# Moving the first two groups' routing matmuls, the first expert's search and loads, and two units' transposes in a fused linear-attention and mixture-of-experts kernel

## The chip, the cores and the metric

The kernel runs on one core of one Trainium2 chip. The metric is the device time of one execution in microseconds (us); the time before is the median of three runs. Engines are named as the profile names them: PE is TensorE (PEld its weight loads), DVE is VectorE, ACT is ScalarE, POOL is GpSimd, and SP is SyncE, which issues most DMA transfers. TensorE runs at one of two clock levels, 2.4 or 1.2 GHz.

## The reference

Two parts follow each other. The first is a linear attention with a decaying state; its output rows are the tokens of the second, a mixture of 8 experts of which each token uses one.

```python
B, H, S, D = 4, 8, 768, 48                    # r, k, v: (B, H, S, D)
for t in range(S):
    cur = einsum('bhd,bhe->bhde', u * k_t, v_t)
    y_t = einsum('bhd,bhde->bhe', r_t, state + cur)
    state = w * state + einsum('bhd,bhe->bhde', k_t, v_t)
x = y as rows                                  # (N = 3072, DM = 384)
logits = x @ w_gate + modality_bias[modality_id]      # 8 experts, 2 modalities
e = argmax(logits); g = softmax(logits)[e]
out[n] = g * (relu(x[n] @ w1[e]) @ w2[e])      # w1: 384 x 1024, w2: 1024 x 384
```

## The kernel before

**Units and iterations.** The attention is cut into 24 units: chunk c of 128 time steps (6 of them) of batch b (4), in the order unit = 4 c + b. A hand-written loop runs over iterations i = 0 to 22, and within an iteration the code itself sets the order of every engine's queue; each engine takes its instructions strictly in that order. Iteration i works on several units at once, in this order on PE: the transposes of the finished rows of unit i - 2 (`raised`, into PSUM tile pxT, only for the units in RAISED = 6 to 11), the transposes of the keys of unit i + 2 (`keys_turned`, pkT), the scores of unit i + 1 (`scores`, psc), then the outputs of unit i (`values`: py from the state and from the masked scores at, then the new state pst, then the small matmuls of `bonus`, line 411).

**The chain of a unit's row.** In iteration i + 1 DVE adds the bonus term to py of unit i (`token`, line 509), ACT squares it and sums (line 524), DVE makes a power-of-two scale of it (ebx and sx, lines 314 and 316), ACT writes the high half of the row as fp16 (`high`, line 557), DVE the low half (`low`, line 561). DVE's queue in an iteration is: token, key scaling kc (line 402), ebx, sx, the two masked score halves at (line 456), low. Low frees one of the two py buffers. The row is then turned: for RAISED units by six PE transposes in iteration i + 2 and one ACT copy (`flipped`, line 585), for the others by a DMA transpose that SP issues at the end of iteration i + 1 (`flip`, line 577).

**Transfers.** SP issues the loads of unit i + 5's transposed inputs (ud) and of unit i + 4's keys and values (kv) in iteration i. Ahead of each stands a read of a value whose only use is the time at which it is there (`pace`): SP goes on to ud when ACT has copied d of unit i, and on to kv when DVE has written sx of unit i - 1.

**Routing.** Units form GROUPS (0 to 3, 4 to 7, 8 to 11, 12 to 15, ...). For a group that ends with unit l, PE makes its `logits` at the end of iteration l + 2 and its `count` (how many tokens go to which expert, and each token's place) at the end of iteration l + 4. DVE's parts, `choose` (pick the expert; it ends with three operations on the sum zs, lines 636 to 640) and `place`, are generators in a list `fills`: one operation of it is emitted at each call of `fill()`, between the large operations. `route(i, d, f)` calls f for the group whose last unit is i - d + 1.

**The first expert.** The biases and the token counts of the two modalities tell the order in which experts are worth loading. `setup2` and `first_order` compute it; ctl holds the result, SP reads it in iteration 6, and loads the first expert's 3 MB of weights in 12 halves (`half`, line 964), two in each of iterations 6 to 11. ACT squares and sums six pieces of them for a scale (`norm`, line 967), PE and DVE make the scale of each matrix (`scales`), and ACT and DVE split each piece into fp16 parts whi (line 998) and wlo (line 1003): piece 0 to 2 in iterations 10 to 12, pieces 3 to 5 at the end of iteration 13. The expert's matmuls are woven in from iteration 13 on (`s_up`, `s_down`), and after the attention the kernel runs expert jobs alone.

Of the kernel before, what the change touches and what calls it, by code (L numbers as in the profile page):

```python
# [9 lines left out]
F32 = mybir.dt.float32  # L10
# [5 lines left out]
ALU = mybir.AluOpType  # L16
# [30 lines left out]
TURNED = range(1, 15)  # L47
RAISED = range(6, 12)
OWNED = range(17, 24)
# [3 lines left out]
EARLY = 3  # L53
ROWS, ENDS = 5 * E, 6 * E + 4
GROUPS = ((0, 4), (4, 8), (8, 12), (12, 16), (16, 19), (19, 22), (22, 24))
MS = ('DVE', 'Activation', 'PE', 'SP', 'Pool')
# [9 lines left out]
class _Kernel:  # L66
# [134 lines left out]
    def setup2(self):  # L201
# [9 lines left out]
        yield  # L211
        pt = self.ps_r.tile([P, 512], F32, tag="r", name="pswg")
        nc.tensor.matmul(pt[:, :1], self.ones, ssq, start=True, stop=True)
# [17 lines left out]
        NTT = NT // P  # L231
        mf, mp = pt[:, 64 : 64 + NTT], c.tile([P, 1], F32, name="modp")
        self.polled = pt, mp, bias
        nc.scalar.activation(mf, mod.rearrange("p (t w) -> p t w", w=2)[:, :, 0], AF.Copy, accum_out=mp)
        yield
        mg = pt[:, 96 : 96 + NTT]
# [360 lines left out]
    def choose(self, u):  # L597
# [36 lines left out]
        yield "oh"  # L634
        zs = col(456)
        nc.vector.reduce_sum(zs, ex, axis=AX.X)
# [68 lines left out]
    def sorted(self, key, ck, n=1):  # L705
# [10 lines left out]
        return perm, rank  # L716

    def first_order(self):

        c, v = self.c, self.nc.vector  # L720
        pt, mp, bias = self.polled
        one = slice(0, 1)
        new = lambda name, shape: c.tile(shape, F32, name=name)
        b2 = bias.rearrange("p (m e) -> p m e", m=2)
        n1, rev, best1, perm = new("n1", [P, 1]), new("rev16", [P, E]), new("best1", [P, E]), new("perm0", [P, E, E])
        self.perm0 = perm
        square = lambda ap: ap.rearrange("p (a b) -> p a b", b=E)
        top, gr = pt[:, 384:386], square(pt[:, 128 : 128 + E * E])
        best0, by, rank, t = (pt[:, o : o + E] for o in range(400, 400 + 4 * E, E))
        self.nc.tensor.matmul(pt[:, 1:2], self.ones, mp, start=True, stop=True)  # L730
        v.reduce_max(top, b2, axis=AX.X)
        yield
        self.nc.scalar.activation(rev, self.rev, AF.Copy, scale=1 / 16)
        self.nc.scalar.activation(rev, self.rev, AF.Copy, scale=1 / 16)
        v.tensor_tensor(best0, b2[:, 0], top[:, :1].to_broadcast([P, E]), ALU.is_equal)
        yield
        self.nc.scalar.copy(n1, pt[:, 1:2])
        v.tensor_tensor(best1, b2[:, 1], top[:, 1:].to_broadcast([P, E]), ALU.is_equal)
        yield
        v.tensor_sub(by, best1, best0)  # L740
        yield
        v.scalar_tensor_tensor(best1, best0, float(NT), rev, ALU.mult, ALU.add)
        yield
        v.scalar_tensor_tensor(rev, by, n1, best1, ALU.mult, ALU.add)
        yield
        v.scalar_tensor_tensor(best0, by, n1, best1, ALU.mult, ALU.add)
        yield
        v.tensor_tensor(gr, rev.unsqueeze(1).to_broadcast([P, E, E]), best0.unsqueeze(2).to_broadcast([P, E, E]), ALU.is_gt)
# [12 lines left out]
        self.nc.scalar.copy(self.ctl[:, :E], eid)  # L761
# [393 lines left out]
    def run(self):  # L1155
# [26 lines left out]
        def plan(step, f):  # L1182
            at.setdefault(step, []).append(f)
# [5 lines left out]

        def half(q):  # L1190
            if q == 0:
                self.eid = nc.sync.value_load(self.ctl[:, :1], min_val=0, max_val=E - 1)
            if 0 <= q < 2 * NQ:
                self.load(self.eid, 2 * NQ, q)

# [4 lines left out]
        def chain(*gs):  # L1200
            for g in gs:
                yield from g

        routing = self.setup2()
        plan(0, lambda: next(routing))
        plan(1, lambda: next(routing))
        plan(1, lambda: fills.append(routing))
        plan(3, lambda: fill(99))
        plan(3, lambda: fills.append(self.first_order()))
        mid[5] = lambda: fill(99)  # L1210
        plan(3, lambda: nc.sync.dma_start(self.ut, self.u.to_broadcast([P, DM])))
        plan(4, lambda: nc.gpsimd.memset(self.st[0], 0.0))
# [7 lines left out]
        for q in range(NQ):  # L1220
            plan(O + 9 + q, norm(q))
        for q in range(3):
            plan(O - 1 + q, norm(q))
        begin[O + 2] = lambda: scales("w1", 0, O + 2)
        for q in range(3):
            plan(O + 2 + q, split(q))
            plan(O + 2 + q, norm(3 + q))
            plan(O + 5, split(3 + q))
        mid[O + 5] = lambda: self.values(O + 5, lambda: (scales("w2", 1, O + 6), self.undo()))
        for q in range(NQ):  # L1230
# [24 lines left out]
        for i in range(NU - 1):  # L1255
# [6 lines left out]
            if i + 1 > EARLY:  # L1262
                each(i + 1, self.own_keys)
            route(i, 3, lambda u: fills.append(self.choose(u)))
            route(i, 5, lambda u: fills.append(chain(self.place(u), self.ahead(ahead[u["lo"]], u)) if u["lo"] in ahead else self.place(u)))
# [24 lines left out]
            if 0 < i < NU - 5:  # L1290
                self.pace(self.ctx_[i]["d"])
                each(i + 5, self.turned)
            half(2 * (i - O) + 4)
            for j in range(2):
# [20 lines left out]
            if i:  # L1315
                fac = self.factor(i - 1)
                for _ in fac:
                    fill()
                if i < NU - 4:
                    self.pace(self.ctx_[i - 1]["g"]["sx"][:, self.ctx_[i - 1]["at_g"] :])  # L1320
                    each(i + 4, self.lines)
                half(2 * (i - O) + 5)
                each(i + 3, self.own_lines)
# [16 lines left out]
            fill()  # L1340
            if i != O + 5:
                self.values(i)
            if up is not None:
# [8 lines left out]
            if i != O + 4 and any(hi - 1 + d == i for lo, hi in GROUPS for d in (4, 5)):  # L1352
                fill(99)
            route(i, 2, self.logits)
            route(i, 4, self.count)
            for f in at.get(i, ()):
# [215 lines left out]
```

## Time and profile before

| | us |
|---|---|
| median of 3 runs (340.3, 342.31, 342.3) | 342.3 |
| the profiled execution, its own time | 340.73 |
| its span, first to last instruction | 338.9 |
| PE busy | 322.9 |
| DVE busy | 210.2 |
| ACT busy | 180.9 |
| POOL busy | 159.7 |

The profiled execution takes 1.8 us more than its span, and stands between the runs. All times of the profile below count from the span's start. Iteration i of the loop begins on PE with the first transposes of that iteration; iterations 1 to 4 take about 3.6 to 5 us each, iterations 5 to 12 about 5 to 8, and the attention's loop ends at about 160 us. The expert jobs fill the rest. A matmul's duration in the profile overlaps the next one's, so what PE needs for a piece of work is read from one start to the next.

### The profile page before, as it was taken

The page shows a single profiled execution, that of the slowest core. Times are in us where ns is not written, and L with a number is a line of the kernel's source. Part 1 is how long each engine was busy: PE and PEld are TensorE (multiplying, and loading weights), DVE is VectorE, ACT ScalarE, POOL GpSimd, SP SyncE. Part 2 cuts the span into 40 slices and gives each one's busy share as a digit, 9 for nine tenths or more (in the row PEclk, how much of TensorE's full clock was granted, in tenths as well). Part 3 has the DMA queues.
Part 4 walks back from the last instruction along what each step waited for, and adds up shares of the span by engine and source line. Part 5 has one row for each costly group of instructions (what it writes and reads, how often), then busy time and mean ns, then how long its engine had stood idle before and what let it go on. Part 6 is the DMA issues. An engine that isn't in the chain of part 4 may idle for free. (4 is left out here: it accounts for less than half of the span.)

```text
span 338.9 us, 15229 instructions
## 1 busy us (share of the span) xinstructions
PE 322.9 (95%) x5450; PEld 263.9 (78%) x5450; DVE 210.2 (62%) x729; ACT 180.9 (53%) x498; POOL 159.7 (47%) x237
## 2 busy tenths in 40 slices
PE   8999899779999999999999999999999999999992
PEld 3889798679869788887877788886888887777771
DVE  8988776588897978787768632267222332334950
ACT  7897698679647568567532222265222224552920
POOL 8988864967948786625358411112122110111211
PEclk9999799989999999999999999999999999999998
DMA  6899996776459999974445542117611121112110
GB/s 184 242 178 189 187 270 191 237 211 184 136 163 220 223 297 302 212 169 104 96 118 188 167 112 51 47 47 261 186 47 47 47 69 24 47 47 70 37 47 5
DMA packets 58013, 47.93 MB, mean 141 GB/s; under 512 B 42344, under 2 KB 50807, under 8 KB 57712
## 3 DMA queue, kind: packets, MB, share of 16 engines
q1 hardware_dynamic: 54768, 37.85, 47.3%
q0 software_dynamic: 3200, 9.47, 7.8%
q8 instruction: 30, 0.49, 0.6%
q14 instruction: 15, 0.12, 0.1%
HBM read 27.21 MB, written 11.83 MB: 115 GB/s over the span
## 5 line engine op out<-in xcount | busy, mean ns | idle before, releaser
L1057 PEld LDWEIGHTS <-whi 128*128 128x128 f16 x1248 | 72.4, 98 | 3.7 <-issue 0.7
L1066 DVE SCALAR_TENSOR_TENSOR hl<-phb,hh 128x256 f16<-128x256 f32 (+1 forms) x48 | 24.4, 508 | 68.4 <-ACTq L1503 68.4
L1120 PEld LDWEIGHTS <-hh 128*128 128x128 f16 x416 | 39.1, 98 | 27.8 <-issue 3.0
L1057 PE MATMUL phb<-mxT,whi 128*128 128x128 f16 x768 | 50.7, 219 | 0.0
L436 ACT ACTIVATE dv<-kv,d 128x48 f32<-128x48 f32 x172 | 43.0, 326 | 0.2 <-DVE d L417 0.2
L1061 ACT ACTIVATE hh<-phb 128x256 f16<-128x256 f32 (+1 forms) x48 | 21.4, 454 | 32.4 <-PE phb L1057 23.2
L1057 PEld LDWEIGHTS <-wlo 128*128 128x128 f16 x624 | 37.7, 98 | 0.0
L1026 POOL TENSOR_TENSOR seenb<-otb,putb 128x1 int32<-128x1 int32 x16 | 4.1, 255 | 64.2 <-ACTq L1503 52.0
L456 DVE TENSOR_TENSOR at<-psc,mask 128x512 f32<-128x512 f32 x48 | 31.8, 681 | 1.1 <-PE psc L450 1.0
L1120 PEld LDWEIGHTS <-hl 128*128 128x128 f16 x208 | 19.4, 98 | 15.3 <-issue 2.5
L364 POOL TENSOR_TENSOR rc<-ud,powr 112x512 f32<-112x512 f32 (+1 forms) x25 | 30.7, 1231 | 1.1 <-PE py L480 0.8
L450 PE MATMUL psc<-rc,kc 64*64 64x128 f32 (+1 forms) x768 | 29.0, 289 | 1.6 <-issue 1.3
L695 POOL DMA_INDIRECT rows<-row,posi x24 | 25.2, 1050 | 11.1 <-DVE base L671 4.1
L1017 ACT ACTIVATE otb<-po,fac 128x384 f32<-128x384 f32 x16 | 9.3, 580 | 39.5 <-PE phb L1057 39.5
L1057 PE MATMUL phb<-mxT,wlo 128*128 128x128 f16 x384 | 29.3, 219 | 0.0
L1120 PE MATMUL po<-whi,hl 128*128 128x384 f16 x136 | 28.0, 326 | 1.2 <-PEq L1568 0.7
L1120 PE MATMUL po<-whi,hh 128*128 128x384 f16 x136 | 27.7, 326 | 0.5 <-ACT hh L1061 0.2
L450 PEld LDWEIGHTS psc<-rc,kc 64*64 64x64 f32 (+1 forms) x768 | 22.3, 140 | 7.2 <-issue 4.2
L1120 PE MATMUL po<-wlo,hh 128*128 128x384 f16 x136 | 27.6, 326 | 0.0
L487 PE MATMUL py<-kv,at 128*64 128x48 f32 x768 | 26.6, 222 | 0.8 <-issue 0.8
L1057 PE MATMUL phs<-mxT,whi 128*128 128x128 f16 x432 | 27.2, 219 | 0.0
L487 PEld LDWEIGHTS py<-kv,at 128*64 128x64 f32 x768 | 25.0, 138 | 1.6 <-issue 1.2
(288 smaller groups left out, 628.2 us busy)
## 6 DMA issues: line engine op xcount, KB each, us to landing
kv<-in_pt SPq DMA_DIRECT2D x21, 384.0 KB, 5.3
ud<-in_pd SPq DMA_DIRECT2D x10, 384.0 KB, 4.1
raw<-in_w SPq DMA_DIRECT2D x12, 256.0 KB, 4.1
raw<-in_w SPq DMA_DIRECT2D x6, 512.0 KB, 5.2
raw<-in_w SPq DMA_DIRECT2D x2, 1536.0 KB, 6.4
ud<-in_pd SPq DMA_DIRECT2D x14, 192.0 KB, 3.7
rows<-pad SPq DMA_DIRECT2D x10, 193.0 KB, 2.6
rt<-in_pt SPq DMA_DIRECT2D x7, 192.0 KB, 5.7
```

What stands on the lines that cost most here:

```text
L364: nc.gpsimd.tensor_mul(u["rc"][:TOP, s], u["rT"][:TOP, s], self.powr[:TOP, s])
L436: nc.scalar.activation(u["dv"][:, sl], u["v"][:, sl], AF.Copy, scale=u["d"][:, h : h + 1])
L450: nc.tensor.matmul(u["ps"][j][s, pr * P : (pr + 1) * P], u["kc"][r, pr, s], u["rc"][r, pr, :], start=True, stop=True)
L456: nc.vector.tensor_mul(u["at"][:, j * NPR : (j + 1) * NPR, :], u["ps"][j].rearrange("p (q t) -> p q t", q=NPR), self.mask.unsqueeze(1).to_ ...
L487: nc.tensor.matmul(py[t, sl], u["at"][:, j * NPR + pr, t], u["v"][:, sl], start=c == h == 0, stop=h == H - 1, skip_group_check=True)
L695: i = nc.gpsimd.indirect_dma_start(out=self.rows, out_offset=bass.IndirectOffsetOnAxis(ap=u["posi"][:, b : b + 1], axis=0), in_=u["row"][: ...
L1017: self.nc.scalar.activation(ot, po[:, :DM], AF.Copy, scale=gf[:, t : t + 1])
L1026: i1 = nc.gpsimd.tensor_tensor(seen, ot[:, 0:1].bitcast(I32), idx, ALU.add)
L1057: self.nc.tensor.matmul(ph[:, q * P : (q + 1) * P], w[:, c0 : c0 + P], self.xT[:, xq, t * P : (t + 1) * P], start=i == q == 0, stop=i == l ...
L1061: self.nc.scalar.activation(self.hh[:, f0 : f0 + fb, t * P : (t + 1) * P], p3, AF.Relu)
L1066: self.nc.vector.scalar_tensor_tensor(self.hl[:, f0 : f0 + fb, r], p3, 0.0, self.hh[:, f0 : f0 + fb, r], ALU.max, ALU.subtract)
L1120: self.nc.tensor.matmul(po[:, :DM], h[:, f, t * P : (t + 1) * P], w[:, c0 : c0 + DM], start=first, stop=last)
```

## The change

Five things are moved or replaced; the arithmetic stays.

- **Logits and counts** of the groups that begin below unit 8 (SOON) are issued one iteration later, behind the scores: the logits of group 0 in iteration 6 and of group 1 in 10, the counts in 8 and 12. DVE's `choose` and `place` stay in the iterations in which they were.
- **zs**, the sum over the exponentials, lies in SBUF, where it was a column of the PSUM tile that the counts write.
- **The first expert** is found by a generator of its own, `first`, which shares iteration 2 and the start of 3 with `setup2`. Nine operations of `first_order` become ten in `first`, two of them small ACT reads of a PE result; the rest of `first_order` follows in iterations 4 and 5. SP reads the expert's number in iteration 3, and the 12 halves are issued in iterations 3 to 10. The load of ut moves from iteration 3 to 13.
- **The pieces**: norms in iterations 5 and 7 to 11 (before 7 to 12); the scale of w1 in iteration 9 (before 10), that of w2 at the start of 12 (before in the middle of 13); splits of pieces 0 to 3 in iterations 9 to 12 and of pieces 4 and 5 in 13.
- **RAISED** begins with unit 4: the rows of units 4 and 5 are turned by PE and copied by ACT, and their two DMA transposes are gone.

```diff
@@ constants
-RAISED = range(6, 12)
+RAISED = range(4, 12)
+SOON = 8
@@ setup2 (the routing's constants, a generator)
-        mf, mp = pt[:, 64 : 64 + NTT], c.tile([P, 1], F32, name="modp")
-        self.polled = pt, mp, bias
-        nc.scalar.activation(mf, mod.rearrange("p (t w) -> p t w", w=2)[:, :, 0], AF.Copy, accum_out=mp)
-        yield
+        mf = pt[:, 64 : 64 + NTT]
@@ choose
-        zs = col(456)
+        zs = new("zs", 1)
@@ new: first (finds the first expert); first_order keeps the rest
+    def first(self):
...
+        nc.scalar.activation(pt[:, 64 : 64 + NT // P], mod.rearrange("p (t w) -> p t w", w=2)[:, :, 0], AF.Copy, accum_out=mp)
+        nc.tensor.matmul(pt[:, 1:2], self.ones, mp, start=True, stop=True)
+        v.reduce_max(top, bias.rearrange("p (m e) -> p m e", m=2), axis=AX.X)
+        yield
+        nc.scalar.copy(n[:, 1:2], pt[:, 1:2])
+        nc.scalar.activation(n[:, 0:1], pt[:, 1:2], AF.Copy, scale=-1.0, bias=float(NT))
+        yield
+        two = [pt[:, 400 + E * m : 400 + E * m + E] for m in range(2)]
+        for m in range(2):
+            v.tensor_scalar(two[m], bias[:, m * E : (m + 1) * E], top[:, m : m + 1], n[:, m : m + 1], ALU.is_equal, ALU.mult)
+            yield
+        v.scalar_tensor_tensor(part, two[0], 16.0, self.rev, ALU.mult, ALU.add)
+        yield
+        v.scalar_tensor_tensor(ck, two[1], 16.0, part, ALU.mult, ALU.add)
+        yield
+        v.reduce_max(best, ck[one], axis=AX.X)
+        yield
+        v.scalar_tensor_tensor(two[0][one], ck[one], best, self.idx[one], ALU.is_equal, ALU.mult)
+        yield
+        v.reduce_sum(e0, two[0][one], axis=AX.X)
+        yield
+        v.tensor_copy(self.ctl[:, :1], e0)
+        v.scalar_tensor_tensor(two[0], two[1], 16.0, part, ALU.mult, ALU.add)
+        yield
@@ run: the loads of the first expert's weights
-        def half(q):
-            if q == 0:
-                self.eid = nc.sync.value_load(self.ctl[:, :1], min_val=0, max_val=E - 1)
-            if 0 <= q < 2 * NQ:
-                self.load(self.eid, 2 * NQ, q)
+        halves = {3: (None, 0), 4: (1, 2), 5: (3, 4), 6: (5,), 7: (6,), 8: (7, 8), 9: (9, 10), 10: (11,)}
+
+        def half(i, at):
+            for q in halves.get(i, ())[at : at + 1]:
+                if q == 0:
+                    self.eid = nc.sync.value_load(self.ctl[:, :1], min_val=0, max_val=E - 1)
+                if q is not None:
+                    self.load(self.eid, 2 * NQ, q)
@@ run: the plan
-        plan(1, lambda: fills.append(routing))
-        plan(3, lambda: fill(99))
-        plan(3, lambda: fills.append(self.first_order()))
+        plan(1, lambda: fills.append(chain(beside(self.first(), routing, 2, 5), routing, self.first_order())))
-        plan(3, lambda: nc.sync.dma_start(self.ut, self.u.to_broadcast([P, DM])))
+        plan(13, lambda: nc.sync.dma_start(self.ut, self.u.to_broadcast([P, DM])))
-        for q in range(3):
-            plan(O - 1 + q, norm(q))
-        begin[O + 2] = lambda: scales("w1", 0, O + 2)
-        for q in range(3):
-            plan(O + 2 + q, split(q))
-            plan(O + 2 + q, norm(3 + q))
-            plan(O + 5, split(3 + q))
-        mid[O + 5] = lambda: self.values(O + 5, lambda: (scales("w2", 1, O + 6), self.undo()))
+        norms = {}
+        for i, q in ((5, 0), (7, 1), (8, 2), (9, 3), (10, 4), (11, 5)):
+            norms.setdefault(i, []).append(q)
+        begin[9] = lambda: scales("w1", 0, 9)
+        begin[12] = lambda: (scales("w2", 1, 12), self.undo())
+        for i, qs in ((9, (0,)), (10, (1,)), (11, (2,)), (12, (3,)), (13, (4, 5))):
+            for q in qs:
+                plan(i, split(q))
@@ run: the loop
             if i + 1 > EARLY:
                 each(i + 1, self.own_keys)
+            route(i, 3, lambda u: u["lo"] < SOON and self.logits(u))
+            route(i, 5, lambda u: u["lo"] < SOON and self.count(u))
             route(i, 3, lambda u: fills.append(self.choose(u)))
...
-            half(2 * (i - O) + 4)
+            half(i, 0)
...
-                half(2 * (i - O) + 5)
+                half(i, 1)
...
-            if i != O + 5:
-                self.values(i)
+            self.values(i)
...
-            route(i, 2, self.logits)
-            route(i, 4, self.count)
+            route(i, 2, lambda u: u["lo"] >= SOON and self.logits(u))
+            route(i, 4, lambda u: u["lo"] >= SOON and self.count(u))
```

Where the instructions stand now is shown at three places. On PE, from the end of iteration 5 into iteration 6, before the change (xT is the turned rows of group 0, pr the logits; one load of weights and one matmul repeat 24 times):

```order
L595 LDWEIGHTS xT_404
L595 MATMUL pr_947<-wghl,xT_404 128x8
L352 MATMUL pkT_972<-id_150,kv_92 112x128 x4
L450 MATMUL psc_0_977<-rc_737,kc_866 64x128
L450 MATMUL psc_1_978<-rc_737,kc_866 64x128
```

And with the change, the first part with the row of unit 4 (row_876) and, after the 32 score matmuls, the first of the logits:

```order
L568 LDWEIGHTS row_876
L568 MATMUL pxT_965<-id_159,row_876 128x128
L350 MATMUL pkT_972<-id_150,kv_92 112x128 x4
L448 MATMUL psc_0_977<-rc_758,kc_890 64x128
L448 MATMUL psc_1_978<-rc_758,kc_890 64x128
...
L593 LDWEIGHTS xT_404
L593 MATMUL pr_997<-wghl,xT_404 128x16
```

The logits have moved from ahead of pkT to behind the scores, and six transposes of unit 4's row stand ahead of pkT.

On DVE in iteration 2, behind the token of unit 1, before the change (kc of unit 4, scale sx of unit 1, masked scores at of unit 3, the low half of unit 1's row):

```order
L402 TENSOR_TENSOR kc_517<-pkT_477,powk 112x512
L314 TENSOR_SCALAR ebx_519<-ssq_405 128x1
L316 TENSOR_SCALAR sx_406<-ebx_519 128x1
L456 TENSOR_TENSOR at_535<-psc_0_482,mask 128x512
L314 TENSOR_SCALAR ebwg<-pswg 128x1
L456 TENSOR_TENSOR at_535<-psc_1_483,mask 128x512
L316 TENSOR_SCALAR wgs<-ebwg 128x1
L561 SCALAR_TENSOR_TENSOR row_403<-py_441,sx_406,row_403 128x384
```

And with the change (npoll is what ACT copies from the PE matmul that sums the modalities, which stands behind the scores of unit 3):

```order
L726 TENSOR_REDUCE btop<-bias 128x2
L733 TENSOR_SCALAR pswg<-bias,btop,npoll 128x8
L400 TENSOR_TENSOR kc_528<-pkT_477,powk 112x512
L312 TENSOR_SCALAR ebx_530<-ssq_405 128x1
L733 TENSOR_SCALAR pswg<-bias,btop,npoll 128x8
L314 TENSOR_SCALAR sx_406<-ebx_530 128x1
L735 SCALAR_TENSOR_TENSOR ckpart<-pswg,idxf 128x8
L454 TENSOR_TENSOR at_547<-psc_0_482,mask 128x512
L737 SCALAR_TENSOR_TENSOR ck_509<-pswg,ckpart 128x8
L454 TENSOR_TENSOR at_547<-psc_1_483,mask 128x512
L739 TENSOR_REDUCE ckbest<-ck_509 1x1
L559 SCALAR_TENSOR_TENSOR row_403<-py_441,sx_406,row_403 128x384
```

An operation that waits for PE's scores, by way of a matmul and two ACT copies, now stands ahead of kc and of sx.

On DVE in iteration 10, before the change (wtotw to winv are the scale of w1, read from a PE matmul, line 982, that stands behind the scores of unit 11):

```order
L819 TENSOR_SCALAR off<-done 128x1
L985 TENSOR_REDUCE wtotw_1595<-py_1469 128x1
L314 TENSOR_SCALAR ebww_1597<-wtotw_1595 128x1
L316 TENSOR_SCALAR ws<-ebww_1597 128x1
L319 TENSOR_SCALAR winv<-ebww_1597 128x1
L402 TENSOR_TENSOR kc_1606<-pkT_1552,powk 112x512
```

With the change it stands in iteration 9, and that iteration ends with the split of piece 0 (the rows between are those of the iteration's row):

```order
L994 TENSOR_REDUCE wtotw_1455<-py_1345 128x1
L312 TENSOR_SCALAR ebww_1457<-wtotw_1455 128x1
L314 TENSOR_SCALAR ws<-ebww_1457 128x1
L317 TENSOR_SCALAR winv<-ebww_1457 128x1
L400 TENSOR_TENSOR kc_1466<-pkT_1406,powk 112x512
...
L834 TENSOR_SCALAR skip<-again_1496 128x1
L1012 SCALAR_TENSOR_TENSOR wlo<-raw,ws,whi 128x1024
L507 TENSOR_TENSOR py_1499<-py_1499,dv_1435 128x384
```

The scale and the first split are one iteration earlier; the splits that follow are spread over one iteration more.

## Rows read from the trace of the kernel before

**Rows 1.** Stretches of the span, us: busy time by engine, PEclk granted clock, DMA.

```profile
30.00:80.60 50.60, 45.30 (x1159) 40.89 (x1157) 38.93 (x129) 39.42 (x126) 36.42 (x38) 0.93 0.87 219
...
100.00:300.00 200.00, 199.44 (x2936) 161.48 (x2936) 111.88 (x433) 87.64 (x226) 76.12 (x132) 1.00 0.52 134
```

**Rows 2.** Waits of PE up to 100 us: releaser, us in total, times, longest.

```profile
PE pr L649 <- DVE row L640: 1.7, 1, 1.7
...
PE pos L1120 <- DVE wlo L1003: 1.4, 2, 0.7
PE psc L450 <- issue: 1.3, 1, 1.3
...
PE pxT L570 <- DVE row L561: 0.4, 1, 0.4
PE pkT L352 <- DMA kv<-in_pt: 0.4, 1, 0.4
```

**Rows 3.** PE in order of time, iterations 5 and 6: start, us, instruction, idle before.

```profile
30.58 1.10 PE L450 MATMUL psc<-rc,kc 64*64 64x128 f32 x32
...
36.63 0.32 PE L595 MATMUL pr<-wghl,xT 128*128 128x16 f16 x6 [0.80 <-DMA xT<-row]
36.81 1.08 PE L352 MATMUL pkT<-id,kv 128*112 128x128 f32 x4
37.82 1.99 PE L450 MATMUL psc<-rc,kc 64*64 64x128 f32 x32
```

**Rows 4.** PE in order of time, iterations 2, 7, 9, 12 and 13.

```profile
19.00 1.14 PE L487 MATMUL py<-kv,at 128*64 128x48 f32 x32
...
44.59 0.88 PE L480 MATMUL py<-st,rc 112*64 112x96 f32 x16
...
47.70 0.26 PE L649 MATMUL pr<-oh,warm 128*128 128x8 f16 x4
...
53.94 0.51 PE L570 MATMUL pxT<-id,row 128*128 128x128 f16 x6
54.29 0.60 PE L352 MATMUL pkT<-id,kv 128*112 128x128 f32 x4
...
74.03 0.71 PE L570 MATMUL pxT<-id,row 128*128 128x128 f16 x6
...
80.61 0.51 PE L570 MATMUL pxT<-id,row 128*128 128x128 f16 x6
```

**Rows 5.** DVE in order of time, iterations 2, 8, 10 and 11.

```profile
18.86 0.15 DVE L316 TENSOR_SCALAR sx<-ebx 128x1 int32<-128x1 int32 x1
...
48.17 0.20 DVE L661 TENSOR_TENSOR pr<-pr,base 128x32 f32<-128x32 f32 x1 [0.90 <-PE pr L653]
...
51.23 0.62 DVE L561 SCALAR_TENSOR_TENSOR row<-py,sx,row 128x384 f16<-128x384 f32 x1
...
63.38 0.16 DVE L985 TENSOR_REDUCE wtotw<-py 128x1 f32<-128x3 f32 x1 [3.41 <-PE py L982]
...
63.89 0.68 DVE L402 TENSOR_TENSOR kc<-pkT,powk 112x512 f32<-112x512 f32 x1
...
66.46 0.60 DVE L561 SCALAR_TENSOR_TENSOR row<-py,sx,row 128x384 f16<-128x384 f32 x1
...
67.30 1.94 DVE L1003 SCALAR_TENSOR_TENSOR wlo<-raw,ws,whi 128x1024 f16<-128x1024 f32 x1
...
73.59 0.59 DVE L561 SCALAR_TENSOR_TENSOR row<-py,sx,row 128x384 f16<-128x384 f32 x1
74.10 1.28 DVE L1003 SCALAR_TENSOR_TENSOR wlo<-raw,ws,whi 128x1024 f16<-128x1024 f32 x1
```

**Rows 6.** SP's issue of the kv load in iteration 2, in order of time.

```profile
19.72 0.39 SPq L343 DMA_DIRECT2D kv<-in_pt  x1
```

**Rows 7.** DMA issues, the page's part 6: KB each, us from issue to landing.

```profile
kv<-in_pt SPq DMA_DIRECT2D x21, 384.0 KB, 5.3
...
raw<-in_w SPq DMA_DIRECT2D x12, 256.0 KB, 4.1
```

**Rows 8.** POOL in order of time, iterations 11 and 12.

```profile
68.37 1.24 POOL L426 TENSOR_TENSOR dv<-kv,d 128x192 f32<-128x192 f32 x1 [0.22 <-ACT d L419]
...
75.74 0.51 POOL L426 TENSOR_TENSOR dv<-kv,d 128x192 f32<-128x192 f32 x1 [2.38 <-ACT d L419]
```

More of the change, by code (lines that the diff above doesn't have):

```diff
@@ L211, in setup2 @@
         yield
-        pt = self.ps_r.tile([P, 512], F32, tag="r", name="pswg")
+        pt = self.polled = self.ps_r.tile([P, 512], F32, tag="r", name="pswg")
         nc.tensor.matmul(pt[:, :1], self.ones, ssq, start=True, stop=True)
@@ L716, in sorted @@
         return perm, rank
+    def first(self):
+        nc, c, v = self.nc, self.c, self.nc.vector
+        _, bias, mod = self.raw_in
+        pt = self.polled
+        new = lambda name, shape, dt=F32: c.tile(shape, dt, name=name)
+        top, n, part, ck, best, e0 = new("btop", [P, 2]), new("npoll", [P, 2]), new("ckpart", [P, E]), new("ck0", [P, E]), new("ckbest", [1, 1]), new("eid00", [1, 1])
+        self.ck0, mp, one = ck, new("modp", [P, 1]), slice(0, 1)
+        nc.scalar.activation(pt[:, 64 : 64 + NT // P], mod.rearrange("p (t w) -> p t w", w=2)[:, :, 0], AF.Copy, accum_out=mp)
[22 more added lines that the diff above has]
+        yield
@@ L718, in first_order @@
     def first_order(self):
-        c, v = self.c, self.nc.vector
-        pt, mp, bias = self.polled
+        c, v, pt = self.c, self.nc.vector, self.polled
         one = slice(0, 1)
         new = lambda name, shape: c.tile(shape, F32, name=name)
[L724 to L748, printed above, removed]
+        perm = self.perm0 = new("perm0", [P, E, E])
@@ L749, in first_order @@
+        gr = pt[:, 128 : 128 + E * E].rearrange("p (a b) -> p a b", b=E)
+        ck, rank, t = (pt[:, o : o + E] for o in (400, 408, 416))
+        v.tensor_tensor(gr, self.ck0.unsqueeze(1).to_broadcast([P, E, E]), ck.unsqueeze(2).to_broadcast([P, E, E]), ALU.is_gt)
         yield
@@ L760, in first_order @@
         yield
-        self.nc.scalar.copy(self.ctl[:, :E], eid)
+        self.nc.scalar.copy(self.ctl[:, 1:E], eid[:, 1:])
         self.settled = new("settled", [P, E])
@@ L1202, in chain, with beside @@
                 yield from g
+        def beside(g, h, lo, n):
+            for k, x in enumerate(g):
+                if lo <= k < lo + n:
+                    next(h)
+                yield x
         routing = self.setup2()
@@ L1221, in run @@
             plan(O + 9 + q, norm(q))
-        for q in range(3):
-            plan(O - 1 + q, norm(q))
-        begin[O + 2] = lambda: scales("w1", 0, O + 2)
-        for q in range(3):
-            plan(O + 2 + q, split(q))
-            plan(O + 2 + q, norm(3 + q))
-            plan(O + 5, split(3 + q))
-        mid[O + 5] = lambda: self.values(O + 5, lambda: (scales("w2", 1, O + 6), self.undo()))
+        norms = {}
[6 more added lines that the diff above has]
+                plan(i, split(q))
+        for i, qs in norms.items():
+            for q in qs:
+                plan(i, norm(q))
         for q in range(NQ):
```

## The prediction

> **What bounds the kernel now.** I read the windows first. From 100 to 300 us TensorE (PE) is busy 199.44 of 200 us [rows 1]: nothing waits there that could be saved, and any microsecond won or lost before 100 us reaches the end whole. From 30 to 80.6 us, the stretch that the change rearranges, PE is busy 45.30 of 50.60 us, at a granted clock of 0.93 [rows 1]. So PE is the bound, with two kinds of loss there: waits, and time at the lower of its two levels.
>
> The table of PE's waits names the losses [rows 2]: 1.7 us for zs at the count of group 0 (L640, read through L649); 1.4 us for two low parts of the weights' pieces (wlo); 0.4 us at pxT for a low half of a row; 0.4 us at pkT for a kv load; and 1.3 us of "issue" that the change gives me no reason to expect gone.
>
> The list in order of time adds the clock. At the logits of group 0 PE waits 0.80 us for the DMA-turned rows xT; just behind it, the four pkT and the 32 score matmuls take 1.08 and 1.99 us where 0.60 and 1.10 are what the same work takes elsewhere [rows 3, 4]: 0.48 + 0.89 = 1.37 us at half clock after a wait. The same follows the 1.7 us wait: the six transposes at 74.03 take 0.71 us, against 0.51 at 53.94 and 80.61 [rows 4]. I put that second fall at the same 1.4 us. Together these are 0.80 + 1.37 + 1.7 + 1.4 + 1.4 = 6.7 us, all of which the change aims at in one way or another.
>
> **Iterations 2 to 8, up to 53.94.** Gone: the wait for xT and its slow stretch, since the logits now stand behind the scores, −2.17. Against that:
>
> First, twelve new transposes for the rows of units 4 and 5. Six cost 54.29 − 53.94 = 0.35 us from start to start [rows 4], so +0.70. Their ACT copies lie beside PE; without that cover the nearest row, DVE's low half over the same 384 columns, gives 0.6 each [rows 5].
>
> Second, iteration 2. On DVE an operation that needs PE's sum of the modalities now stands ahead of kc and sx, and that matmul stands behind the scores of unit 3. Those end at about 19.00, when the next matmuls begin [rows 4]; DVE wrote sx at 18.86 [rows 5]. A matmul, two small ACT copies and the DVE operation follow; the nearest small operations take 0.15 or 0.16 us [rows 5], so I estimate 0.75 with the handing over: 19.75. Then come kc (0.68 [rows 5]), ebx, sx and one more small operation: sx at 20.8 at the earliest, some 2 us late, and the masked scores with it. SP waits for that sx before it issues kv, at 19.72 before [rows 6]: 1.1 to 1.2 us later. The load takes 5.3 us to land [rows 7], and PE had already waited 0.4 us for a kv at pkT [rows 2], so there is no slack. From below the price is 0 (PE, itself held by the late masked scores, gets to pkT later anyhow and recovers that in iteration 3, where DVE has less to do); from above 2.0, the whole delay of sx. I take 0.7, somewhat over half of the load's delay.
>
> Third, what DVE does behind PE's moved work. DVE's operation on a count (`place`) stands ahead of kc and the row's chain. Before, the count ended an iteration, when DVE had time. Now it comes behind the scores, and DVE's whole chain starts there. From the first operation of `place` to the end of the low half, DVE took 48.17 to 51.23 + 0.62 = 3.68 us; with the scale of w1 in iteration 10 (63.38 to 66.46 + 0.60) also 3.68 [rows 5]. PE has less than that: from the matmuls behind the scores to its end of iteration 47.70 − 44.59 = 3.11 us, and 0.17 more since half of the six transposes read only the high half [rows 4]. So PE waits 0.40 at the next pxT each time; the 0.4 us wait at pxT in [rows 2] is this very case. It arises behind the logits of group 0 (iteration 6, found at the transposes of iteration 7) and behind its count (8, found in 9): +0.8. From below 0, where DVE's ready work overlaps; from above twice that.
>
> Stretch: −2.17 + 0.70 + 0.7 + 0.8 = 0.0, bounds −1.5 to +2.1.
>
> **Iterations 9 to 11.** Before, these took 74.03 − 53.94 = 20.09 us [rows 4], 1.7 of it the wait for zs. zs in SBUF removes that wait. But the scale of w1, three splits and two rows' chains now follow one another on DVE. From the start of iteration 9: PE needs 0.35 + 0.60 + 1.10 = 2.05 us for transposes, pkT and scores [rows 3, 4] until DVE can start on the scale; 3.68 to the low half; 0.4 for the small routing operations; the split of piece 0, 1.6 (1.28 to 1.94 [rows 5]); iteration 10: a token (as wide as a low half, 0.60), then 3.68 with the logits of group 1 in place of the scale, and 0.1 between; iteration 11 as before from one split to the low half, 67.30 to 73.59 + 0.59 = 6.88 [rows 5], 0.15 less because PE starts with the high half. Sum 18.9, against 20.09: −1.2. PE alone would need 20.09 − 1.7 − 0.4 = 18.0, so the bounds are −2.1 and, with another chain wait of 0.4 and the slower splits, −0.2.
>
> One rule of the notes speaks against the early split. First the rows: the split took 1.94 us while POOL's dv took 1.24 (68.37), and 1.28 us while POOL, after 2.38 us idle, did its dv in 0.51 (75.74) [rows 5, 8]. The Trainium skill, "SBUF — State Buffer", section "Who interferes with whom", says that a DVE instruction with two inputs in SBUF contends with a GpSimd instruction that reads SBUF; the two rows agree. By it all the pieces moved to iterations where POOL works would cost the longer time, 0.3 us above my 1.6 for piece 0.
>
> **Iteration 12.** Before 80.61 − 74.03 = 6.58 us with a slow stretch [rows 4]. Now the scale of w2 stands at its start and the count of group 1 behind its scores: 2.05 + 0.25 for the matmul behind the scores, 3.68 of chain, and 0.5 for three small operations more at 0.16: 6.4 to 6.6. The slow stretch's 1.4 is replaced by a chain: 0, bounds −1.4 and +0.8.
>
> **Iterations 13 and 14.** The two waits for wlo, 1.4 us in all [rows 2], fall away, since only two pieces are left to iteration 13 and the scale of w2 is there earlier: −1.4, bounds −1.4 to 0.
>
> At nothing: zs in SBUF as a write; the load of ut (its one reader is POOL, for later units); two DMA transposes fewer on SP. The raw halves, 256 KB and 4.1 us to landing each [rows 7], are issued earlier beside kv, at a mean DMA share of 0.87 [rows 1]; I take them as hidden, and their price otherwise is a rival.
>
> **Sum**: 0.0 − 1.2 + 0 − 1.4 = −2.6. The profiled execution's own time, 340.73, is its span of 338.9 and 1.8 around it: it would be 338.1. It lies 1.6 below the median of 342.3, which gives 339.7 for the median.
>
> **The rivals.** *DVE keeps up* (0.34): the chains do not bind, because in the new places PE has other work to cover them. Then all 6.7 us go and only the transposes come: −6.0, 336.3. For it: DVE has 50.60 − 38.93 = 11.7 us free in this stretch [rows 1]. Against: its operations stand in a fixed order, and 3.68 is over 3.28.
>
> *The clock falls again* (0.18): with chains in iteration 11 as computed, PE still waits about as long ahead of the transposes of iteration 12 as it did for zs, and the slow stretch stays behind it: −2.6 + 1.4 = −1.2, 341.1. For it: both slow stretches before followed a wait [rows 2, 3]; against: other waits of 0.4 left no such mark.
>
> *Late keys and values, slower* (0.12): SP issues one or two raw halves in each of iterations 3 to 6, where there was none before 6. At a DMA share of 0.87 [rows 1] 256 KB ahead of kv's 384 may lengthen kv's 5.3 us by up to the half's own 4.1 [rows 7]; 1.5 us of it reaching pkT in each of iterations 4 to 7 would be +6.0 over the forecast, 345.7. It decides from the point where kv lands over 1 us later than its pkT; against it, these iterations were not the busiest for the DMA engines when 12 halves were loaded from 6 to 11.
>
> **How the numbers follow.** My forecast has 0.36, and is the likeliest; its own range is 338.2 to 341.5. It and the falling clock lie within 1% of 342.3 (3.4 us, about what a measurement of this kernel tells from no change): 0.54. Faster by over 1%: 0.34. Slower: 0.12. The range reaches down to the case in which DVE keeps up, 336.0, and up to 344.4, where the upper bounds of the chains and the slow clock add up, and short of late keys in full.
>
> **What would show it.** After the change: no wait at pr for xT, and pkT and scores of iteration 6 near 0.60 and 1.10; sx of unit 1 near 20.8 and kv issued behind it; waits at pxT for row L559 (low) in iterations 7 and 9 to 12; a start of iteration 12 some 18.9 us behind that of 9; no wait for wlo in 14. The forecast is wrong if pxT never waits (then faster), if pkT waits for kv in several iterations (slower), or if PE shows slow stretches at new places.

## The result, and the profile after

The changed kernel takes 345.85 us (median of 6 runs, 344.24 to 346.8), the kernel before on the same chip 342.22 (338.67 to 343.95): 1.0113 times as long, 95% interval 1.0071 to 1.0155. It is slower, and 1.45 us above the range. The profiled execution has a span of 343.9 us against 338.9.

The start of PE's transposes in an iteration, before [rows 4] and after, tells in which stretch the 5.0 us arose:

| start of | before | after | after − before | change in the stretch |
|---|---|---|---|---|
| iteration 9 | 53.94 | 52.55 | −1.39 | −1.39 |
| iteration 12 | 74.03 | 76.07 | +2.04 | +3.43 |
| iteration 13 | 80.61 | 85.72 | +5.11 | +3.07 |
| scores of unit 16 (iteration 15) | 99.88 | 102.86 | +2.98 | −2.13 |
| end of the span | 338.9 | 343.9 | +5.0 | +2.0 |

The loss sits in iterations 9 to 12, and is larger there than the table shows, since the pause of 1.3 us of "issue" (PE waiting for nothing that the profile shows) that lay in iteration 10 before the change [rows 2] is gone. The last row is partly a pause of 1.1 us of "issue" at 139 us; a second profiled execution of the changed kernel (span 343.0) does not have it. PE's waits up to 100 us, after the change (releaser, us in total, times, longest):

```profile
PE pxT L568 <- ACT row L555: 4.6, 2, 3.3
PE pxT L568 <- DVE row L559: 2.3, 4, 1.4
...
PE py L478 <- DVE row L559: 0.8, 2, 0.6
```

The waits for zs, kv and wlo [rows 2] and for xT [rows 3] are gone. In their place stand 6.9 us at the transposes (pxT), for the high halves (ACT, L555) and the low halves (DVE, L559). PE in order of time shows where (start, us, instruction, idle before):

```profile
58.66 0.34 PE L568 MATMUL pxT<-id,row 128*128 128x128 f16 x3 [0.20 <-DVE row L559]
...
65.59 0.34 PE L568 MATMUL pxT<-id,row 128*128 128x128 f16 x3 [1.34 <-ACT row L555]
66.29 0.34 PE L568 MATMUL pxT<-id,row 128*128 128x128 f16 x3 [0.36 <-DVE row L559]
...
67.00 1.98 PE L448 MATMUL psc<-rc,kc 64*64 64x128 f32 x32
...
76.07 0.34 PE L568 MATMUL pxT<-id,row 128*128 128x128 f16 x3 [3.30 <-ACT row L555]
77.77 0.50 PE L568 MATMUL pxT<-id,row 128*128 128x128 f16 x3 [1.35 <-DVE row L559]
78.06 1.06 PE L350 MATMUL pkT<-id,kv 128*112 128x128 f32 x4
79.05 1.99 PE L448 MATMUL psc<-rc,kc 64*64 64x128 f32 x32
```

Iterations 11 and 12 begin late, and behind the 3.30 us wait pkT and the scores run at half clock (1.06 and 1.99 us against 0.60 and 1.10 [rows 3, 4]). The scores of iteration 11 do so too (67.00, 1.98 us), behind waits of 1.34 and 0.36 us. ACT squares a row and writes its high half only when DVE's token has finished it, so both waits lead to DVE. DVE in order of time:

```profile
59.05 3.33 DVE L1012 SCALAR_TENSOR_TENSOR wlo<-raw,ws,whi 128x1024 f16<-128x1024 f32 x1
62.30 0.55 DVE L507 TENSOR_TENSOR py<-py,dv 128x384 f32<-128x384 f32 x1
...
66.60 5.79 DVE L1012 SCALAR_TENSOR_TENSOR wlo<-raw,ws,whi 128x1024 f16<-128x1024 f32 x1
72.31 0.55 DVE L507 TENSOR_TENSOR py<-py,dv 128x384 f32<-128x384 f32 x1
...
77.64 1.27 DVE L1012 SCALAR_TENSOR_TENSOR wlo<-raw,ws,whi 128x1024 f16<-128x1024 f32 x1
```

The splits of pieces 0 and 1, the same instruction that takes 1.27 us at 77.64, take 3.33 and 5.79 us, and the next row's token (py<-py,dv) stands behind them. POOL in the same stretch:

```profile
66.43 1.02 POOL L369 TENSOR_TENSOR kt<-kv,wtok 128x384 f32<-128x384 f32 x1
67.38 1.28 POOL L387 TENSOR_TENSOR rk<-rc,kc 112x512 f32<-112x512 f32 x1
68.61 0.52 POOL L424 TENSOR_TENSOR dv<-kv,d 128x192 f32<-128x192 f32 x1
69.07 1.27 POOL L362 TENSOR_TENSOR rc<-ud,powr 112x512 f32<-112x512 f32 x1
70.30 1.00 POOL L369 TENSOR_TENSOR kt<-kv,wtok 128x384 f32<-128x384 f32 x1
71.25 1.18 POOL L675 COPY row<-tok 128x4 int32<-128x4 int32 x1
75.24 1.27 POOL L387 TENSOR_TENSOR rk<-rc,kc 112x512 f32<-112x512 f32 x1 [2.80 <-DVE ebx L312]
```

No row from 67.38 to 71.25 has idle time in front: POOL works off a backlog. DVE's split ends at 72.39, 1.1 us after the kt that ended at 71.3, and the small copy at 71.25 takes 1.18 us. The same pattern in small was in [rows 8]: a split beside a dv of 1.24 us.

### The profile page after: what moved, and what is told of

The parts are those of the page before. It is cut to its first block, busy times and chain, and to the rows that moved or that the text cites. A ratio compares the mean times of both kernels' runs of the same rounds, so it can differ in the third digit from the quotient of the medians.

```text
span 343.9 us, 15251 instructions
## 1 busy us (share of the span) xinstructions
PE 325.0 (94%) x5462; PEld 266.0 (77%) x5462; DVE 216.4 (63%) x732; ACT 181.8 (53%) x499; POOL 161.1 (47%) x237
## 5 line engine op out<-in xcount | busy, mean ns | idle before, releaser
L1012 DVE SCALAR_TENSOR_TENSOR wlo<-raw,ws,whi 128x1024 f16<-128x1024 f32 (+1 forms) x20 | 31.5, 1593 | 1.5 <-issue 0.7
```

The source lines that it names most:

```text
L1012: self.nc.vector.scalar_tensor_tensor(self.wlo[:, sl], self.raw[:, sl], sc, self.whi[:, sl], ALU.mult, ALU.subtract)
```

## The experiments

**Theory A**: a DVE instruction with two operands in SBUF cannot start while POOL goes from one operation on SBUF data to the next; it then stands for the rest of POOL's backlog. **Rival B**: DVE's chain is too long by itself, or the splits' data are slow to read while raw halves land. Later **rival D**: POOL's backlog is the loss wherever DVE stands. All ratios are to the kernel before on the same chip.

**One operand out of SBUF.** For pieces 0 and 1 (`soon` is the row whose py tile is in use at that place):

```diff
-        self.nc.vector.scalar_tensor_tensor(self.wlo[:, sl], self.raw[:, sl], sc, self.whi[:, sl], ALU.mult, ALU.subtract)
+        near = self.whi[:, sl]
+        if q < 2 and self.soon:
+            near = self.soon["py"][:, :1].to_broadcast([P, sl.stop - sl.start])
+        self.nc.vector.scalar_tensor_tensor(self.wlo[:, sl], self.raw[:, sl], sc, near, ALU.mult, ALU.subtract)
...
```

> The changed kernel, but for pieces 0 and 1 the split's second operand is a PSUM column (of the row's tile py, repeated 1024 times) where it was whi: one operand in SBUF, same place, same size, same output. It leaves out the low parts of these two pieces (their wlo holds something else). Theory A (two operands in SBUF need what POOL holds): both splits take about 1.3 us while POOL runs on without a gap, and the time is 338 to 341. Rival B (the split waits or is slow for another reason: raw halves landing, order, the clock): they stay at 3 to 6 us, time 345 to 347.

Measured: 343.36 us, ratio 1.0029 (0.9988 to 1.0070). DVE, in order of time:

```profile
59.34 1.28 DVE L1015 SCALAR_TENSOR_TENSOR wlo<-raw,ws,py 128x1024 f16<-128x1024 f32 x1
...
65.08 1.27 DVE L1015 SCALAR_TENSOR_TENSOR wlo<-raw,ws,py 128x1024 f16<-128x1024 f32 x1
...
69.90 2.16 DVE L636 SCALAR_TENSOR_TENSOR zs<-zs,sx 128x4 f32<-128x4 f32 x1
```

POOL beside the two splits:

```profile
59.37 1.02 POOL L369 TENSOR_TENSOR kt<-kv,wtok 128x384 f32<-128x384 f32 x1
...
65.77 1.01 POOL L369 TENSOR_TENSOR kt<-kv,wtok 128x384 f32<-128x384 f32 x1
```

Both splits take 1.3 us, in the same place, reading the same raw piece, with POOL busy throughout. Rival B falls for them. The time came down less than theory A said, and the third row tells why: another operation, of 4 columns, now takes 2.16 us. It is the one on zs, and since the change put zs into SBUF, it too has both operands there (0.16 us with zs in PSUM, as the run with zs back there shows below).

**POOL waits for the splits of pieces 0 and 1.** `rest` is a helper of the kernel: POOL copies what it is given into a spare cell, and so waits until that has been written.

```diff
-            v.tensor_copy(self.gap, of)
+            v.tensor_copy(self.gap, of[:1])
...
             for q in qs:
                 plan(i, split(q))
+                if i in (9, 10):
+                    plan(i, lambda q=q: self.rest(self.wlo[:, (q + 1) * WQ - 1 : (q + 1) * WQ]))
```

> The changed kernel, with one tiny POOL copy behind each of the splits of pieces 0 and 1 (iterations 9 and 10), which reads a cell of the split's result: POOL waits there until DVE has written wlo. Nothing else changes. Theory A (POOL's uninterrupted run of two-input operations keeps the split's DVE instruction from starting): the two splits take 1.3 us each where the changed kernel has 3.33 and 5.79; the waits of PE at the transposes of iterations 11 and 12 (1.34 + 0.36 and 3.30 + 1.35) fall to under 1 us each, the half clock behind them goes, and the time falls by 5 to 8 us from 345.85, to 338 to 341. Rival B (the chain of DVE's operations is what is too long, or the pieces' data are slow to read while raw halves land): POOL's waiting gives nothing, the splits stay over 3 us, and the time is 345 to 347.

Measured: 348.36 us, ratio 1.0183 (1.0124 to 1.0242), so the time went the wrong way for both theories. DVE and then POOL:

```profile
65.57 1.31 DVE L1012 SCALAR_TENSOR_TENSOR wlo<-raw,ws,whi 128x1024 f16<-128x1024 f32 x1
...
70.44 6.36 DVE L636 SCALAR_TENSOR_TENSOR zs<-zs,sx 128x4 f32<-128x4 f32 x1
```

```profile
70.11 0.50 POOL L424 TENSOR_TENSOR dv<-kv,d 128x192 f32<-128x192 f32 x1
...
75.79 0.98 POOL L369 TENSOR_TENSOR kt<-kv,wtok 128x384 f32<-128x384 f32 x1
83.92 1.28 POOL L387 TENSOR_TENSOR rk<-rc,kc 112x512 f32<-112x512 f32 x1 [7.15 <-DVE posi L667]
```

The splits fell to 2.10 and 1.31 us. Only the first fell because POOL waited: the copy behind piece 1 (at 68.74) found nothing to wait for, since that split had already started at 65.57, just ahead of POOL's pause before a scatter at 65.95. And the operation on zs took the place: 6.36 us for 128x4, until POOL's kt ended at 76.77. PE waited 6.9 us at 78.04 for the low half behind it. Theory A holds for the instruction, but I had looked at two victims only.

**A POOL operation that reads nothing.** A memset in place of the waiting copy:

```diff
+                if i in (9, 10):
+                    plan(i, lambda: nc.gpsimd.memset(self.hl[:, :4], 0.0))
```

> The changed kernel, with a POOL memset of 128 x 1024 fp16 at the two places at which the run before has its waiting copies; it reads nothing and waits for nothing, so that POOL only has more to do. Theory A, if it is POOL's reads that keep DVE out: the split of piece 1 starts under the memset and takes about 2 us (0.8 until the memset starts, 1.3 of its own), not 5.79, and the time falls by 3 us or more. Rival B, and theory A if any POOL instruction keeps DVE out: the split takes 5.8 us or more and the time is 346 or above.

Measured: 343.23 us, ratio 1.0039 (0.9988 to 1.0091): POOL has more to do, and the ratio is below the changed kernel's 1.0113, though the intervals overlap. POOL and DVE around piece 0:

```profile
59.14 1.00 POOL L369 TENSOR_TENSOR kt<-kv,wtok 128x384 f32<-128x384 f32 x1
60.08 0.95 POOL L1247 MEMSET hl<- 128x1024 f16 x1
60.99 1.38 POOL L387 TENSOR_TENSOR rk<-rc,kc 112x512 f32<-112x512 f32 x1
```

```profile
59.15 2.09 DVE L1012 SCALAR_TENSOR_TENSOR wlo<-raw,ws,whi 128x1024 f16<-128x1024 f32 x1
...
65.46 1.29 DVE L1012 SCALAR_TENSOR_TENSOR wlo<-raw,ws,whi 128x1024 f16<-128x1024 f32 x1
```

The split of piece 0 ends at 61.24, that is 1.1 us after kt's end at 60.14: it ran beside the memset, where in the changed kernel it had to let rk pass too (3.33). This is one place only. That the split of piece 1 is short is no effect of its memset: it came early enough to start in POOL's pause of 0.17 us before a scatter at 65.50. It was what I expected the memset to do, so that point is not tested.

**Parts alone.** The pieces as before, all else changed:

> The changed kernel with norms, scales and splits of the pieces where the kernel before has them (scale of w1 in iteration 10, splits in 10 to 12 and three in 13, scale of w2 in 13); all else (logits and counts behind the scores, zs in SBUF, first expert early, raw halves early, rows 4 and 5 by PE) as changed. Theory A: no split in iteration 9, so the loss there goes; the split of piece 0 in iteration 10 meets POOL at work and takes 1.3 to 6 us according to whether POOL has a gap; the two waits for wlo in iteration 14 (1.4 in all) are back: 339 to 343. Rival B, if the moved logits and counts or the early loads were the loss: 344 to 347.

Measured: 350.34 us, 1.0196 (1.0092 to 1.0299): slower than either theory said. The kernel before with only logits and counts moved, with zs in SBUF and with zs in PSUM:

> The kernel before with two parts of the change alone: logits and counts of groups 0 and 1 behind the scores one iteration later, and zs in SBUF. First expert, halves, pieces and the rows of units 4 and 5 as before. Prediction's steps: the wait for xT (0.80) with its half clock (1.37) and the wait for zs (1.7) go; a wait of about 0.4 us at a low half behind each moved piece of work comes: ratio 0.985 to 1.0. Theory A adds that zs and its operands in SBUF meet POOL's run at 68 to 73 us: the operation on zs takes 0.6 us or more (0.16 before), up to 6 us if POOL has no gap, and then the ratio is 1.0 to 1.015.

> The kernel before with the logits and counts of groups 0 and 1 behind the scores alone, zs in PSUM as before. Theory A: the operation on zs stays at 0.16 us; the count, an iteration later, no longer waits for zs; the wait for xT goes: ratio 0.980 to 0.998. If the moved logits and counts are themselves a loss (DVE's chain behind the scores is longer than what PE has to do), the ratio is 1.0 to 1.01 with waits of 1 us and more at the transposes of iterations 7, 9, 11 and 13.

Measured: 345.05 us, 1.0176 (1.0098 to 1.0254), and 345.21 us, 1.0122 (1.0056 to 1.0188). Both are slower than anything expected of them (at most 1.015 and 1.01), though by less than the intervals. The split of piece 0 in the run with the pieces late, and in the one with logits and counts alone and zs in PSUM:

```profile
64.77 6.64 DVE L1012 SCALAR_TENSOR_TENSOR wlo<-raw,ws,whi 128x1024 f16<-128x1024 f32 x1
```

```profile
64.09 6.60 DVE L1004 SCALAR_TENSOR_TENSOR wlo<-raw,ws,whi 128x1024 f16<-128x1024 f32 x1
```

So the early split is not needed for the loss. In the last run the scores of unit 12 begin at 64.60, 3.2 us earlier than before (67.82): the moved routing gains what it should. Then the split comes earlier into POOL's backlog, waits longer, and PE waits 5.6 us for the next row. With zs in SBUF (the other run) the split took 1.87 and the operation on zs 0.58 us; 3.1 of the 3.2 us by which it was behind at the scores of unit 12 arose before the scores of unit 8, with pauses of PE and half clock that no theory here covers; that is left open.

**Both victims freed, then all.** The two POOL waits and zs back in PSUM (`zs = col(456)`):

> The changed kernel with POOL waiting for the splits of pieces 0 and 1, as in the run that only did this, and with zs back in the PSUM tile of the counts (column 456), so that DVE's operation on zs and sx has one operand in SBUF again. Theory A (any DVE operation with two operands in SBUF, however small, is kept out by POOL's uninterrupted run): no split over 2.2 us, the operation on zs at 0.2 us where the run with zs in SBUF had 6.36, the wait of 6.9 us at the transposes of iteration 12 under 2.5 us, and the time 3 to 8 us below that run: 341 to 345 if the clock still falls once, 338 to 341 if not. Rival C (POOL's late work itself is what holds the rows, so that a pause for POOL has to cost): the operation is short but PE waits as long for another reason, and the time is 346 or above.

Measured: 343.63 us, 1.0137 (1.0060 to 1.0214). DVE:

```profile
70.53 0.16 DVE L636 SCALAR_TENSOR_TENSOR pr<-pr,sx 128x4 f32<-128x4 f32 x1
...
71.79 6.14 DVE L1012 SCALAR_TENSOR_TENSOR wlo<-raw,ws,whi 128x1024 f16<-128x1024 f32 x1
```

The operation on zs is at 0.16 us, and now the split of piece 2 takes 6.14. PE's matmul of the scale of w2 waits 3.8 us for ACT's square of the row behind it. So "no split over 2.2 us" failed, at a third place. Rival C, by which a pause of POOL has to cost, asked for 346 us or above; 343.63 speaks against it. Turning units 4 and 5 by DMA instead, in the same kernel:

> The run with POOL's waits and zs in PSUM, and the rows of units 4 and 5 turned by DMA again (raised units from 6 on). Prediction's step: twelve transposes are 0.70 us on PE and with them the waits for low halves at the transposes of iterations 6 and 7 (0.35) go: 0.7 to 1.1 us faster than that run, if the DMA-turned rows of group 0 are there when the logits come behind the scores of iteration 6. Rival: the logits wait for them again (0.3 us or more, with half clock behind), and nothing is won.

Measured: 342.8 us, 1.0081 (1.0035 to 1.0128), 0.8 us less than the run before it and so as expected, though the intervals overlap. The 6.14 us split is the same. Then POOL waits for all four splits (`if i in (9, 10, 11, 12)`, zs in PSUM), with the changed kernel itself beside it, and the same with units 4 and 5 turned by DMA (`RAISED = range(6, 12)`):

> The changed kernel unchanged, on the same chip as the runs beside it, so that these can be compared with it. All theories: 1.005 to 1.016 times the kernel before; one DVE instruction with two operands in SBUF of over 5 us between 60 and 75 us.

> The changed kernel with POOL waiting for each of the splits of pieces 0 to 3 (iterations 9 to 12) and zs in PSUM; against the run with two such waits and zs in PSUM, only the waits behind pieces 2 and 3 are new. Theory A (one instruction with two operands in SBUF is kept out for as long as POOL works off its backlog, and it is the next such instruction that is hit when one is freed): the split of piece 2, 6.14 us there, takes under 2.6; the wait of 3.8 us at the scale of w2 in iteration 12 and the half clock behind it go; span 335 to 338, ratio 0.980 to 0.997. Rival D (the backlog of POOL itself is the loss, and will stop PE at some place whatever DVE does): PE waits 3 us or more at another place, for POOL's rk or rc, and the ratio stays at 1.005 to 1.015.

> The same with the rows of units 4 and 5 turned by DMA. Theory A: as the run beside it, less what twelve transposes and the waits at them cost: 0.5 to 1.1 us below it, ratio 0.977 to 0.995. Rival D: 1.005 or above.

Measured, on one chip: the changed kernel 345.03 us, 1.0115 (1.0073 to 1.0157), with the 5.79 us split again; all four waits 339.03 us, 1.0023 (0.9978 to 1.0068); with units 4 and 5 by DMA 337.91 us, 0.9877 (0.9821 to 0.9934). The gain over the changed kernel is firm: the twelve runs with all four waits go from 337.06 to 341.63 us, the changed kernel's twelve from 343.99 to 348.56, and the medians are 6.0 us apart. The ratios to the kernel before are not: its 29 runs on this chip go from 335.92 to 354.4 us, and the two ratios lie 1.5% apart where the two medians lie 0.3% apart. So 1.0023, which missed theory A's 0.980 to 0.997 and rival D's 1.005 to 1.015 alike, and 0.9877 both say "about the kernel before or a little faster", and no more.

DVE, PE and POOL of the last, and a stretch of it and of the changed kernel:

```profile
58.62 2.11 DVE L1012 SCALAR_TENSOR_TENSOR wlo<-raw,ws,whi 128x1024 f16<-128x1024 f32 x1
...
64.96 1.32 DVE L1012 SCALAR_TENSOR_TENSOR wlo<-raw,ws,whi 128x1024 f16<-128x1024 f32 x1
...
71.13 2.17 DVE L1012 SCALAR_TENSOR_TENSOR wlo<-raw,ws,whi 128x1024 f16<-128x1024 f32 x1
```

```profile
52.24 0.60 PE L568 MATMUL pxT<-id,row 128*128 128x128 f16 x6
...
70.18 0.34 PE L568 MATMUL pxT<-id,row 128*128 128x128 f16 x3
71.27 0.34 PE L568 MATMUL pxT<-id,row 128*128 128x128 f16 x3 [0.76 <-DVE row L559]
...
77.63 0.34 PE L568 MATMUL pxT<-id,row 128*128 128x128 f16 x3
```

```profile
60.80 0.18 POOL L683 CAST gap<-wlo 1x1 f32<-1x1 f16 x1 [1.16 <-PE pr L593]
...
68.15 0.18 POOL L683 CAST gap<-wlo 1x1 f32<-1x1 f16 x1
...
72.17 1.18 POOL L675 COPY row<-tok 128x4 int32<-128x4 int32 x1
73.44 0.18 POOL L683 CAST gap<-wlo 1x1 f32<-1x1 f16 x1
```

```profile
60.00:75.00 15.00, 11.08 (x278) 10.03 (x268) 13.79 (x24) 7.65 (x23) 12.06 (x12) 0.89 0.51 147
...
60.00:75.00 15.00, 12.27 (x326) 10.83 (x324) 13.38 (x40) 12.19 (x33) 13.72 (x16) 1.00 0.80 190
```

No split of pieces 0 to 3 is over 2.2 us (one of the two in iteration 13 takes 3.9, and PE does not wait for it), and no wait at the transposes is over 0.8. In the stretch from 60 to 75 us (busy time of PE, PEld, DVE, ACT, POOL, then granted clock; the changed kernel first) the clock stays at 1.00, where it was 0.89, with POOL busy 13.72 of 15 us, where it was 12.06. PE waits once for POOL's rk, 0.5 us: rival D, that POOL's backlog stops PE in any case, falls. Of the four added copies only those behind pieces 0 and 3 stood idle (1.16 us, and 2.5 at 79.98). The split of piece 2 got in at the copy of tok ahead of the third (72.17, 1.18 us), where in the run with two waits it did not (that copy took 0.18). So the added copy changed this, but no row shows how. The run with all waits but without the DMA turning had a span of 340.0, with two pauses of PE ("issue") of 1.3 and 1.8 us in it; how much of the 1.1 us between the two medians is the twelve transposes, as expected, these runs do not tell.

Last, the routing alone with POOL's waits:

> The kernel before with the logits and counts of groups 0 and 1 behind the scores (zs in PSUM, all else as before), and POOL waiting for the splits of pieces 0, 1, 2 in iterations 10 to 12. The same without POOL's waits was 1.012 times the kernel before, with a split of 6.60 us. Theory A: that split takes under 2.6 us, the 5.6 us wait at the transposes of iteration 11 is under 1 us, ratio 0.975 to 0.995. Rival D: 1.0 or above, PE waiting for POOL instead.

Measured: 341.87 us, 0.997 (0.9926 to 1.0015), against 1.0122 without the waits. In the profiled execution, a long one at 344.64 us, the split takes 2.76 us where it took 6.60, and the wait at the transposes is 1.5, not under 1. So theory A was right in direction, but its 0.975 to 0.995 was missed: this kernel is not faster than the kernel before beyond the interval.

## Why the prediction was wrong, point by point

**The step that failed** is the term for the split in "Iterations 9 to 11": "the split of piece 0, 1.6 (1.28 to 1.94 [rows 5])", and iteration 11 "as before from one split to the low half, 67.30 to 73.59 + 0.59 = 6.88 [rows 5]". They measured 3.33 us and, from 66.60 to the low half's end at 77.71, 11.1. I took two durations from the profile of before as the two ends of the cost. But the 1.94 was no upper bound. That split owed it to a pause of 0.22 us that POOL made in front of its dv at 68.37 [rows 8], waiting for ACT, and that was luck; nor is it the longest in the profile of before (ns: shortest, median and longest of the 20 splits):

```profile
L1003 DVE SCALAR_TENSOR_TENSOR wlo<-raw,ws,whi x20: 746/1279/2161, 67.3 to 321.6; 128x1024 f16<-128x1024 f32 x16, 128x512 f16<-128x512 f32 x4
```

What bounds the split is, at most places, the time until POOL pauses, and POOL's rows of before could have told how long that can be. From 55.83 to 73.36 us POOL had no pause above 0.3 us.

Around that term the total came out. Iterations 9 to 12 were predicted at 18.9 + 6.6 = 25.5 us; the run with all splits freed and units 4 and 5 by DMA takes 77.63 − 52.24 = 25.4, the changed kernel 85.72 − 52.55 = 33.2. That it is so close is partly luck: iterations 9 to 11 take 17.9 there (70.18 − 52.24) and iteration 12 7.5 (the terms for 9 to 11 add up to 18.84, not 18.9). The 6.0 us that separate the changed kernel from the one with all four waits are about what the forecast missed, 345.85 − 339.7 = 6.15.

**The rule that spoke against the change.** I had cited the Trainium skill, "SBUF — State Buffer", "Who interferes with whom", and priced it at 0.3 us a piece. The same page of the Trainium skill, "Summary: rules for kernel authors", says that when DVE has two inputs in SBUF and the GpSimd operation reads SBUF, the second to issue is fully blocked until the first finishes. The traces agree that it blocks, that one operand in PSUM avoids it (1.28 us), and that a POOL operation that only writes lets it pass (the memset). They differ in the length: the splits of 5.79 to 6.64 us stood for five to seven POOL operations, not one.

**"At nothing: zs in SBUF as a write"** was the second miss. It put a second operand into SBUF: 6.36 us in one run, 2.16 in another, 0.58 in the changed kernel itself.

**Iteration 12**, predicted at no change, took 3.07 us longer: 1.35 for the low half, 1.3 for a longer stretch at half clock, which reaches on over the outputs (1.55 and 1.71 us at 81.39 and 82.72 where 0.88 and 1.09 are full speed). That the clock falls again there was a rival; it came with a longer wait than I gave it.

**Iterations 2 to 8** were predicted at 0.0 and gained 1.39. Right: DVE's operation that waits for the modalities' sum at 19.79 (predicted 19.75), sx at 20.83 (20.8), kv issued at 21.14 (1.4 late, predicted 1.1 to 1.2), iteration 5 at 30.84 (+0.84, predicted +0.7), a wait of 0.35 at the low half of iteration 7 (0.40). But the 0.84 arose otherwise: PE waited 0.64 us for a low half that frees a py buffer, not for kv. The second low wait, 0.40 in iteration 9, did not come, and two pauses of "issue" of 0.3 and 0.8 us in the profile of before are absent: 1.1 of the 1.39 us is luck.

**Iterations 13 and 14**: −1.4 predicted; −2.13 up to the scores of unit 16. The waits for wlo are gone.

**The rivals.** "Late keys and values" gives 345.7, close to the measured time, by a mechanism that did not occur: pkT waits for kv nowhere, and kv lands in 3.9 us where it took 5.3 [rows 7]. "DVE keeps up" falls with the waits at pxT. The case that came about, a DVE instruction held out by POOL, was not priced as a rival, though a row and a rule for it stood in the text.

## What to carry to other kernels

When DVE work is moved, list its instructions with two SBUF operands and lay them beside POOL's queue: what counted here was not POOL's busy share but its next pause, and a profile's longest duration of such an instruction is no bound for another place. A cheap cure is to make POOL wait for the DVE instruction, for every such instruction in the stretch, since freeing one hands the wait to the next; another is to keep one operand in PSUM, also for a tile of four columns. And a gain ahead of a stretch that a third engine bounds is given back there: the routing's 3.2 us were (1.0122), and with POOL's waits its ratio was 0.997.

## What the runs showed that I had not expected

- A small DVE instruction is held as long as a large one: one of 128x4 took 6.36 us, those of 128x1024 took 5.79 to 6.64.
- A handover from one POOL operation to the next did not let DVE in at most places, though in some it did: at 61.24 and 71.25 us in the changed kernel the split got in, and POOL's dv and copy there took 1.50 and 1.18 us instead of some 0.5 and 0.2. What tells these places apart is open.
- It repeats: two profiled executions of the changed kernel, on different runs, have the same 3.33 and 5.79 us.
